# Storing the last two half-groups in parts of 88 and 40 partitions

## The chip, the core and the metric

The kernel runs on one core of a Trainium2 chip. The core has TensorE (PE) for matrix products, VectorE (DVE), ScalarE (ACT) and GpSimd (POOL) for elementwise work, SyncE (SP), which here only issues transfers, and 16 DMA engines that move bytes between the chip's HBM and the on-chip memory SBUF, which has 128 partitions. Every time is device time in microseconds (us), of one whole execution. The kernel before takes 258.17 us, the median of three runs (257.88 to 258.88).

## The reference

Two stages, an attention through 49 agents and a feed-forward layer with a maximum of three products:

```python
def _attn_ref(q, k, v, agents):          # q, k, v: 4 x 12544 x 128, agents: 4 x 49 x 128, float32
    def sm(a, b):                        # softmax of scaled products
        s = scale * (a @ b.transpose(0, 2, 1))
        ...
    agent_v = sm(agents, k) @ v
    return sm(q, agents) @ agent_v

def _moe_ref(x, w1, w2, w3, w_out):      # x: the 50176 rows of the above; w: 128 x 768, w_out: 768 x 128
    h = np.maximum(np.maximum(x @ w1, x @ w2), x @ w3)
    return h @ w_out
```

q, k, v and the output are 25.7 MB each. The output has 50,176 rows of 128 float32.

## The kernel before, in words

Work is cut into tiles of 128 rows: 98 for each of the 4 batches. For each batch, steps of seven tiles of k and v are loaded, cast to bf16 on POOL (for the first batch's v on ACT), turned on PE, and summed into the 49 agents' values. From these the feed-forward layer's products are worked out for each batch once, in the 49 agents rather than in the rows (names nr, pu, pv ... gy).

Then come 49 steps over q, numbered s = 0 to 48. Step s takes a group of eight tiles (the last step, 48, takes the two tiles left over in each batch). A step casts q on POOL (qc), turns it on PE (qt) and copies it out on ACT (qe), multiplies with the agents (sc), exponentiates (ex), sums (su), inverts the sums (re), forms hidden values (u, a, v, x) and the output products (p), and scales these by the inverse sums into an SBUF tile OS: `ov.s.0` writes tiles 0 to 3 of the group, `ov.s.1` tiles 4 to 7. Both run on DVE, but for `ov.47.1`, which runs on ACT as four ACTIVATEs of one tile each (L571), beside DVE's `ov.47.0` (L568).

All large transfers are issued by SyncE on one queue: 40 loads of k and v, 17 of q, 4 of weights and 20 stores, 81 in all, each with all 128 partitions of its tile. The agents alone, 49 partitions, are loaded from ACT's queue (L209). Stores, in `store` (L491 to L498), take three groups at a time (1,536 KB) as long as s is below 45. Steps 45, 46 and 48 are stored alone (512 KB each). Step 47, the last that is worked on, is stored in halves of 256 KB: `st.47.1` after `ov.47.1`, then `st.47.0` after `ov.47.0`. In a half, each partition holds four rows of the output that lie next to each other in HBM, so a partition's part is one run of 4 x 128 x 4 = 2,048 bytes.

The order of all work on all engines is written out by hand in a table of names (`ORDER`), which ends with `st.46 st.47.1 st.47.0`. The names carry the places of their buffers. Eight completion semaphores for transfers (DMAHW0 to DMAHW7) are handed out in turn, so a transfer waits until the one eight issues before it has landed. If too many hidden units stay undecided, another branch (`in_general`) would be taken; it isn't with these inputs. At the end SyncE waits at L754 until each of the eight semaphores shows that its last transfer has landed, and all engines meet in a barrier.

Of the kernel before, what the change touches and what calls it, by code (L numbers as in the profile page):

```python
# [16 lines left out]
P, H, C, A, B, NT, GT, KT, NF = 128, 64, 128, 49, 4, 98, 8, 7, 6  # L17
# [176 lines left out]
class Emit:  # L194
# [296 lines left out]
    def store(self, s, h=None):  # L491
        def fn():
            n = LONG if s < NQ - 1 - TG else GT
            far, near = self.far("out", s, n), self.near(s, self.t[f"os.{s // TG * TG}"], n)
            if h is not None:
                far, near = (x[:, self.tiles(s, h), :] for x in (far, near))
            self.nc.sync.dma_start(far, near)
        return fn  # L498

# [259 lines left out]
```

## Time and profile before

| | |
|---|---|
| median of three runs | 258.17 us |
| the profiled execution | 257.99 us, its span 256.2 us |
| busy share: PE, DVE, ACT, POOL | 76%, 63%, 56%, 57% |
| moved on the large queue q1 | 104.34 MB in 12,432 packets |
| HBM read and written | 78.74 MB, 25.69 MB |
| over the span | 408 GB/s |

The profile is of one execution. Its times count from the span's start. A DMA share of 1.00 means that all 16 DMA engines are moving bytes. A packet is what one DMA engine moves in one go; a transfer's packets are its partitions' runs of bytes, and one mark of 4 bytes on each engine that took part, by which the transfer's semaphore is raised when that engine is done. SPq, ACTq and so on are the instruction streams' own steps (issues and waits), which don't count as an engine's busy time. In a row of a stretch the columns are the stretch, its length, the busy time of PE, PE's weight loads, DVE, ACT and POOL, the clock granted to PE, the DMA share and GB/s.

### The profile page before, as it was taken

What the parts mean: (1) busy time and instruction counts of PE and PEld (TensorE: products, weight loads), DVE (VectorE), ACT (ScalarE), POOL (GpSimd) and SP (SyncE); (2) the same over time, 40 slices, a digit from 0 to 9 for tenths busy, and PEclk for the clock granted to TensorE, in tenths of its full rate; (3) what the DMA queues carried; (4) which work ended last, traced back from release to release, by engine and by line L of the source; (5) the groups of instructions that cost most, each with busy time, mean ns of one, the idle gap of its engine ahead of it and who ended that gap; (6) DMA issues with size and microseconds to landing.
All of it is one profiled execution on the core that took longest, in us unless ns stands there. A gap on an engine that the chain in (4) does not pass through costs nothing.

```text
span 256.2 us, 8245 instructions
## 1 busy us (share of the span) xinstructions
PE 193.7 (76%) x3441; PEld 146.3 (57%) x3441; DVE 160.4 (63%) x332; ACT 144.0 (56%) x240; POOL 144.9 (57%) x164
## 2 busy tenths in 40 slices
PE   0676676889999569997892998559596699999800
PEld 0565555676778348775672586447475376565400
DVE  5353323658788578887647686807448668888820
ACT  2463455654876567573842675237282568888610
POOL 2414533998788498946864496384791663414000
PEclk9995777599999999999995699959899689999965
DMA  6999999999999999999999999999999999999993
GB/s 259 431 417 421 411 432 422 423 420 417 421 418 428 426 423 420 421 425 423 414 429 430 422 421 430 420 424 427 423 430 425 420 422 427 428 425 406 408 387 128
DMA packets 12682, 105.05 MB, mean 410 GB/s; under 512 B 1304, under 2 KB 2524, under 8 KB 4572
## 3 DMA queue, kind: packets, MB, share of 16 engines
q1 hardware_dynamic: 12432, 104.34, 97.3%
q8 instruction: 29, 0.48, 0.7%
q10 hardware_dynamic: 203, 0.10, 0.2%
q14 instruction: 18, 0.14, 0.1%
HBM read 78.74 MB, written 25.69 MB: 408 GB/s over the span
## 4 chain that ended last, share of the span: by engine, by line
DMA 51%; PE 22%; ACT 9%; POOL 7%; issue 4%; DVE 2%; ACTq 0%; DVEq 0%; POOLq 0%
DMA LD<-in_q_dram 32%; PE psum L271 16%; DMA LD<-in_v_dram 13%; PE psum L303 7%; DMA LD<-in_k_dram 6%; ACT QT L514 4%; POOL VB L298 3%; POOL QB L508 2%; DVE OS L568 2%; ACT AS L547 1%; POOL KB L298 1%; ACT VB L296 1%; ACT EQ L527 1%; ACT w_bf L347 1%; ACT EK L318 1%
## 5 line engine op out<-in xcount | busy, mean ns | idle before, releaser
L508 POOL CAST QB<-LD 128x1024 bf16<-128x1024 f32 x49 | 50.0, 1055 | 48.6 <-DMA LD<-in_q_dram 42.6
L298 POOL CAST KB<-LD 128x896 bf16<-128x896 f32 x56 | 51.2, 947 | 27.4 <-DMA LD<-in_k_dram 25.2
L568 DVE TENSOR_TENSOR OS<-psum,RC 128x512 f32<-128x512 f32 x97 | 61.4, 678 | 8.4 <-PE psum L271 5.7
L514 ACT ACTIVATE QT<-psum 128x1024 bf16<-128x1024 bf16 x49 | 50.2, 1024 | 26.2 <-PE psum L303 26.0
L309 DVE COPY KT<-psum 128x896 bf16<-128x896 bf16 x56 | 34.4, 620 | 38.4 <-PE psum L303 37.5
L298 POOL CAST VB<-LD 128x896 bf16<-128x896 f32 x42 | 38.6, 951 | 8.2 <-DMA LD<-in_v_dram 8.2
L303 PE MATMUL psum<-ident,QB 128*128 128x128 bf16 x392 | 34.5, 239 | 11.0 <-POOL QB L508 11.0
L303 PEld LDWEIGHTS <-QB 128*128 128x128 bf16 x392 | 28.9, 108 | 23.0 <-POOL QB L508 12.5
L527 ACT ACTIVATE EQ<-psum 128x512 bf16<-128x512 f32 x49 | 29.3, 598 | 21.3 <-PE psum L271 19.9
L303 PE MATMUL psum<-ident,KB 128*128 128x128 bf16 x392 | 36.4, 246 | 6.3 <-POOL KB L298 5.8
L271 PE MATMUL psum<-QT,agT 128*128 128x512 bf16 (+1 forms) x104 | 32.6, 403 | 8.7 <-ACT QT L514 8.3
L318 ACT ACTIVATE EK<-psum 128x343 bf16<-128x343 f32 x56 | 24.9, 460 | 25.3 <-PE psum L271 19.7
L550 DVE TENSOR_TENSOR R<-psum,AS 128x512 bf16<-128x512 f32 x49 | 32.7, 678 | 7.1 <-ACT AS L547 6.6
L303 PEld LDWEIGHTS <-KB 128*128 128x128 bf16 x392 | 28.2, 111 | 10.8 <-POOL KB L298 8.3
L547 ACT ACTIVATE AS<-psum 128x512 bf16<-128x512 f32 x49 | 28.6, 600 | 9.5 <-PE psum L271 9.3
L271 PE MATMUL psum<-EQ,G 128*128 128x512 bf16 (+1 forms) x104 | 31.9, 379 | 0.0
L271 PEld LDWEIGHTS <-EQ 49*128 49x128 bf16 (+1 forms) x588 | 20.9, 96 | 11.1 <-ACT EQ L527 4.6
L271 PE MATMUL psum<-EK,VB 128*128 128x49 bf16 x392 | 19.7, 187 | 5.6 <-ACT VB L296 3.9
L271 PEld LDWEIGHTS <-ones 128*128 128x128 bf16 x417 | 17.8, 98 | 8.1 <-issue 3.1
L271 PE MATMUL psum<-EK,ones 128*128 128x49 bf16 x392 | 19.6, 187 | 2.2 <-ACT EK L318 2.2
L271 PE MATMUL psum<-G,EQ 49*128 49x128 bf16 x392 | 19.9, 220 | 0.5 <-DVE OS L568 0.5
L271 PE MATMUL psum<-G,R 64*128 64x128 bf16 x392 | 19.3, 217 | 0.5 <-DVE R L550 0.2
(82 smaller groups left out, 186.9 us busy)
## 6 DMA issues: line engine op xcount, KB each, us to landing
LD<-in_q_dram SPq DMA_DIRECT2D x16, 1536.0 KB, 18.8
out_dram<-OS SPq DMA_DIRECT2D x15, 1536.0 KB, 22.4
LD<-in_k_dram SPq DMA_DIRECT2D x16, 1344.0 KB, 16.7
LD<-in_v_dram SPq DMA_DIRECT2D x16, 1344.0 KB, 17.1
LD<-in_k_dram SPq DMA_DIRECT2D x4, 896.0 KB, 18.5
LD<-in_v_dram SPq DMA_DIRECT2D x4, 896.0 KB, 17.6
out_dram<-OS SPq DMA_DIRECT2D x3, 512.0 KB, 10.4
LD<-in_moe_w_dram SPq DMA_DIRECT2D x3, 384.0 KB, 12.9
```

The costliest lines, as they stand in the source:

```text
L271: self.nc.tensor.matmul(out, w, x, start=start, stop=True, skip_group_check=True)
L296: self.nc.scalar.activation(out, src, AF.Copy)
L298: self.nc.gpsimd.tensor_copy(out=out, in_=src)
L303: self.nc.tensor.transpose(t[:, j * P:(j + 1) * P], src[:, j, :], self.ident)
L309: return lambda: self.nc.vector.tensor_copy(out=self.t[f"kT{r}"], in_=self.t[f"kT_ps{r}"].bitcast(BF16)[:, :KT * C])
L318: return lambda: self.nc.scalar.activation(self.t[f"e{r}"], self.t[f"s{r}"][:, :KT * A], AF.Exp, scale=SCALE)
L508: return lambda: self.nc.gpsimd.tensor_copy(out=self.t[f"qb.{s}"], in_=self.half("q", s))
L514: return lambda: self.nc.scalar.activation(self.t[f"qT.{s}"].rearrange("p j c -> p (j c)"), self.t[f"qT_ps.{s}"].bitcast(BF16), AF.Copy)
L527: return lambda: self.nc.scalar.activation(self.t[f"e.{s}"], self.t[f"qs.{s}"], AF.Exp, scale=SCALE)
L547: return lambda: self.nc.scalar.activation(self.t[f"a.{s}"], self.t[f"u.{s}"], AF.Relu)
L550: return lambda: self.nc.vector.tensor_tensor(out=self.t[f"r.{s}"], in0=self.t[f"v.{s}"], in1=self.t[f"a.{s}"], op=ALU.max)
L568: self.nc.vector.tensor_tensor(out=out, in0=src, in1=rc.unsqueeze(2).to_broadcast([P, 4, C]), op=ALU.mult)
```

## The change

The two stores with a half given (`st.47.1` and `st.47.0`) are each issued as two transfers, partitions 0 to 87 and then 88 to 127, with the same bytes in all. `h` is given for these two alone.

```diff
@@ -494,6 +494,9 @@
             far, near = self.far("out", s, n), self.near(s, self.t[f"os.{s // TG * TG}"], n)
             if h is not None:
                 far, near = (x[:, self.tiles(s, h), :] for x in (far, near))
+                for rows in (slice(0, 88), slice(88, P)):
+                    self.nc.sync.dma_start(far[rows], near[rows])
+                return
             self.nc.sync.dma_start(far, near)
         return fn
```

No other engine's order changes; lines behind L496 are numbered three higher. On SyncE, at the end of the branch that runs, OS_115 is the tile of steps 45 to 47, `128x1024` is a group and `128x512` a half; in brackets stands what a transfer waits for. Before:

```order
L497 DMA out_dram<-OS_117 128x4x256 [waits DMAHW2_49,DVE_49]
L497 DMA out_dram<-OS_116 128x3072 [waits DMAHW3_49,DVE_49]
L497 DMA out_dram<-OS_118 128x3072 [waits DMAHW4_49,DVE_49]
L497 DMA out_dram<-OS_114 128x3072 [waits DMAHW5_49,DVE_49]
L497 DMA out_dram<-OS_115 128x1024 [waits DMAHW6_49,DVE_49]
L497 DMA out_dram<-OS_115 128x1024 [waits DMAHW7_49,DVE_49]
L497 DMA out_dram<-OS_115 128x512 [waits DMAHW0_49,Activation_49]
L497 DMA out_dram<-OS_115 128x512 [waits DMAHW1_49,DVE_49]
L258 UNCONDITIONAL_BRANCH
```

With the change:

```order
L500 DMA out_dram<-OS_117 128x4x256 [waits DMAHW2_49,DVE_49]
L500 DMA out_dram<-OS_116 128x3072 [waits DMAHW3_49,DVE_49]
L500 DMA out_dram<-OS_118 128x3072 [waits DMAHW4_49,DVE_49]
L500 DMA out_dram<-OS_114 128x3072 [waits DMAHW5_49,DVE_49]
L500 DMA out_dram<-OS_115 128x1024 [waits DMAHW6_49,DVE_49]
L500 DMA out_dram<-OS_115 128x1024 [waits DMAHW7_49,DVE_49]
L498 DMA out_dram<-OS_115 88x512 [waits DMAHW0_49,Activation_49]
L498 DMA out_dram<-OS_115 40x512 [waits DMAHW1_49]
L498 DMA out_dram<-OS_115 88x512 [waits DMAHW2_49,DVE_49]
L498 DMA out_dram<-OS_115 40x512 [waits DMAHW3_49]
L258 UNCONDITIONAL_BRANCH
```

Each half has become two rows. The second half's first part takes the semaphore DMAHW2 instead of DMAHW1 and so waits for the store of step 48 (`128x4x256`), and the part behind it takes DMAHW3 and waits for the store after that. The second part of a half waits for no engine, since the first part ahead of it has already done so.

## The prediction

> **What bounds the kernel now.** I read the page's overview of 40 slices first, to see which resource is full over the whole span and which at its end.
>
> ```profile
> span 256.2 us, 8245 instructions
> DMA  6999999999999999999999999999999999999993
> GB/s 259 431 417 421 411 432 422 423 420 417 421 418 428 426 423 420 421 425 423 414 429 430 422 421 430 420 424 427 423 430 425 420 422 427 428 425 406 408 387 128
> ```
>
> The DMA engines are at nine tenths in every slice but the first and the last; moving bytes bounds the kernel. The change touches only the last slice, so I went to its end: the timeline of the three engines that still work there (SPq rows are transfers being issued; third column is the duration, rows of several are merged).
>
> ```profile
> 243.30 1.88 DVE L568 TENSOR_TENSOR OS<-psum,RC 128x512 f32<-128x512 f32 x3
> 243.90 1.14 ACT L571 ACTIVATE OS<-psum,RC 128x128 f32<-128x128 f32 x4 [1.25 <-PE psum L271]
> 244.60 0.33 SPq L497 DMA_DIRECT2D out_dram<-OS  x1
> 245.07 1.14 SPq L497 DMA_DIRECT2D out_dram<-OS  x1
> 246.31 0.97 SPq L497 DMA_DIRECT2D out_dram<-OS  x1
> ```
>
> VectorE and ScalarE finish at 245.2 and 245.0. The last two rows are the two half-group stores: issued from 245.07 and 246.31, the second done issuing at 247.28. What happens between there and 256.2 is shown by the DMA issues of the stretch from 246.25 on (KB, then us from issue to landing) and SyncE's waits there.
>
> ```profile
> out_dram<-OS SPq DMA_DIRECT2D x1, 256.0 KB, 8.6
> ...
> SPq L754 <- DMA out_dram<-OS: 7.5, 2, 6.7
> ```
>
> The last store lands 8.6 us after its issue began, at 246.31 + 8.6 = 254.9; SyncE waits 7.5 us for such landings; 1.3 us of closing follow. 256 KB at the pace of the full slices is well under a microsecond, so nearly all of the 8.6 us is queueing behind earlier stores. How the queue drains decides the case. The stretches of the tail (the last two columns are the DMA share and GB/s; nothing else is busy):
>
> ```profile
> 246.00:248.00 2.00, 0.00 (x0) 0.00 (x0) 0.00 (x0) 0.00 (x0) 0.00 (x0) 0.50 0.99 396
> 250.00:252.00 2.00, 0.00 (x0) 0.00 (x0) 0.00 (x0) 0.00 (x0) 0.00 (x0) 0.50 0.68 269
> 252.25:253.00 0.75, 0.00 (x0) 0.00 (x0) 0.00 (x0) 0.00 (x0) 0.00 (x0) 0.50 0.30 117
> 253.00:253.25 0.25, 0.00 (x0) 0.00 (x0) 0.00 (x0) 0.00 (x0) 0.00 (x0) 0.50 0.28 107
> 253.25:253.75 0.50, 0.00 (x0) 0.00 (x0) 0.00 (x0) 0.00 (x0) 0.00 (x0) 0.50 0.19 74
> 253.75:254.25 0.50, 0.00 (x0) 0.00 (x0) 0.00 (x0) 0.00 (x0) 0.00 (x0) 0.50 0.09 37
> 254.25:256.20 1.95, 0.00 (x0) 0.00 (x0) 0.00 (x0) 0.00 (x0) 0.00 (x0) 0.50 0.00 0
> ```
>
> Times 16, the shares count the engines still working: 16 to 248, about 11 from 250 to 252, 5 from 252.25 to 253, 3 around 253.5, one or two up to 254.25, none after. The 16 engines do not finish together; about five end by 250, six around 252.2, five between 253.1 and 254.2. The kernel ends when the last of them does. Bytes per working engine stay the same throughout: 396 / (0.99 x 16) = 25.0 GB/s at the start, 74 / (0.19 x 16) = 24.3 near the end. A lone engine gets no faster, so a row of 2,048 bytes costs its engine 2,048 / 25.0 = 82 to 2,048 / 24.3 = 84 ns, at any time.
>
> **The change part by part.** First, on how many engines a transfer runs. The table of queues:
>
> ```profile
> q1 hardware_dynamic: 12432, 104.34, 97.3%
> q8 instruction: 29, 0.48, 0.7%
> q10 hardware_dynamic: 203, 0.10, 0.2%
> ```
>
> q10 carries one transfer alone, the agents, 49 partitions with 4 rows of 512 bytes each: 196 packets. 203 - 196 = 7 are left, the completion marks, one for each engine that took part. So 49 partitions went over 7 engines. On q1 each of the 81 transfers (61 loads, 20 stores, all of 128 partitions) leaves 16 marks: 81 x 144 packets, and 2 x 384 more for the two transfers with four rows a partition, are 12,432. The pattern that fits both is the largest number up to 16 that divides the partitions. By it 88 partitions go over 11 engines with 8 rows each, 40 over 10 engines with 4 rows each. This is worked out, not shown: neither shape occurs before.
>
> *Rows on an engine.* A half-group store gave each of 16 engines 8 rows. It now gives ten engines 8 + 4 = 12, one engine 8 and five none, if the smaller sets lie within the larger. Two halves: 8 more rows for ten engines, 0 for one, 16 fewer for five. At 83 ns: +0.66 us, 0, and -1.33 us. There are also two more marks on each of ten engines; of 4 bytes each, I cost them at nothing, with 0.02 us as the upper end.
>
> *Which engine is last.* Five engines are within 1.1 us of the end and the very last, on its own, within some 0.4 us. If it is one of the ten, everything behind it moves by +0.66 us. No view names engines; by count that is 10 of 16.
>
> *Two more issues on SyncE.* A usual issue is 0.33 us (244.60 row); the last two took 1.14 and 0.97. Four issues at 1.14 and about 0.1 us between them end at 245.07 + 4 x 1.24 = 250.0. The engine that ends at 254.2 begins the rows of the last two stores 16 x 0.083 = 1.3 us earlier, at 252.9. So 2.9 us of queued work cover the issues on that engine and I cost them at nothing; if that backlog were gone, the cost would be up to 250.0 - 247.28 = 2.7 us. The engines that run dry by 250 may wait for rows, but have four microseconds to spare.
>
> *Waits.* SyncE's order, shown with the change above, has each transfer wait for the one issued eight before it (its DMAHW semaphore). The second half's wait moves from DMAHW1 to DMAHW2 and its second part waits for DMAHW3, which the store five places ahead of the first half signals. That store's issue, and its time to landing:
>
> ```profile
> 226.19 0.34 SPq L497 DMA_DIRECT2D out_dram<-OS  x1
> ...
> out_dram<-OS SPq DMA_DIRECT2D x1, 1536.0 KB, 16.9
> ```
>
> It lands at 226.19 + 16.9 = 243.1, two microseconds before the first half is issued, and DMAHW2 was issued before it. No new stall. No compute engine waits for these stores, and nothing moves on PE, ACT, DVE or POOL.
>
> *Sum.* 0.66 + 0 + 0 + 0 = +0.66 us, bounds -1.3 (all five late engines spared) and +0.68. The profiled execution took 257.99 us around its span of 256.2, 0.18 under the median 258.17; the span would be 256.9, and the median 258.8.
>
> A rule that speaks against this change: the Trainium skill ("DMA: Bandwidth & Descriptors", section Rules for kernel authors) says not to split a transfer over disjoint sets of partitions, since both parts spray across all 16 engines and serialize. The 7 marks of q10 speak against the "all 16" for a part whose partitions 16 does not divide; by the rule as it stands the change would be a mere second issue, with next to no cost.
>
> **The rivals.**
>
> *The last engine is spared.* If it is one of the five left out, it ends at 254.2 - 1.3 = 252.9 and the next ones decide. The rows have about three working engines until 253.75, so some still end around 253.8; with +0.66 they end at 254.4 to 254.5: +0.25 us, 258.4. For it: 5 in 16 by count; against it: two or three of the late ones would have to be spared before it brings more. The Trainium skill (same page, section Latency and other measured facts) says that engines 7 and 15 are usually slower; if the last one here were 15, this rival would be it. No row here can tell, and I leave a fair chance for it.
>
> *All five late engines are spared.* On the other side of zero: they end by 252.9, the six of 252.2 become last at 252.2 + 0.66 = 252.9, and the gain is 254.2 - 252.9 = 1.3 us: 256.9. It decides only where the set of five left out is the set of five late ones. Instruction fetches (q8: 0.7% of 16 engines' 256.2 us, 29 us in all) could make some engines late and not others, but that picks out no such set.
>
> *The parts go over all 16 engines.* 88 rows are at most 6 on an engine, 40 at most 3: 9 rows for 8, +0.17 us in two halves, 258.3. Against it: 203 packets on q10.
>
> *Slower rows or fewer engines.* Ten or eleven engines might read the same part of SBUF against each other, and no row before has such a store. If the 24 rows on an engine took half as long again, that is +1.0 us more: 259.8. If the number of engines has to be a divisor of 16, both parts go over 8, 16 rows for 8: +1.33 us, 259.5. The seven of q10 speak against the second; the first stays open.
>
> **How the numbers follow.** Last engine among the ten: 0.60, its 10 in 16 with a little taken off for the mechanisms that no row shows. Last one spared: 0.20. All 16: 0.05. All five spared: 0.03. Slower rows or fewer engines: 0.12. I predict the likeliest, 258.8. The range 258.2 to 259.5 leaves out the 0.03 below, part of the 0.12 above, and some room for the median, whose runs spread from 257.88 to 258.88. 0.5%, about what a measurement of this kernel can tell from no change, is 1.3 us: below 256.9 lies hardly half of the five-spared case (0.02); above 259.46 lie most of the slower rows and a little of the first case (0.13); the rest, 0.85, is the same.
>
> **What would show it.** On the page of the changed kernel q1 has 12,432 - 32 + 2 x (11 + 10) = 12,442 packets; 12,464 would mean 16 engines each, 12,432 eight. The issues show two of 176 KB and two of 80 KB in place of two of 256. In the tail the shares should fall below 11 engines from 248 on sooner, and the last working stretch should reach 254.9 in place of 254.2, with the closing 1.3 us unchanged. SyncE's last issue should end by 250. The prediction is wrong if an issue of the last four stands in a wait for a landing, if a row of 2,048 bytes costs other than 83 ns on a working engine, or if the late engines turn out to be the spared ones.

## The result and the profile after

The changed kernel takes 258.47 us (median of 20 runs, 258.04 to 259.04), the kernel before 257.92 us (20 runs beside them, 257.48 to 258.88). The ratio is 1.0022, 95% interval 1.0016 to 1.0028: +0.57 us, between 0.41 and 0.72. It is slower, by less than half a percent. The forecast was +0.66 us. The 258.8 us named with it stood on 258.17 for the kernel before, whose median over these 20 runs is 257.92.

The profiled execution has a span of 256.8 us in place of 256.2. The lines on the span, on the two queues that told how many engines take part, and on the four last issues (those without a third number have no time to landing there):

```profile
span 256.8 us, 8209 instructions
...
q1 hardware_dynamic: 12442, 104.34, 97.2%
...
q10 hardware_dynamic: 203, 0.10, 0.1%
...
out_dram<-OS SPq DMA_DIRECT2D x2, 176.0 KB
out_dram<-OS SPq DMA_DIRECT2D x2, 80.0 KB
```

q1 has ten packets more, as worked out beforehand: two transfers fewer with 16 marks, two more with 11 and two with 10. A sum of packets can't tell 11 and 10 from another pair with the same sum, but the landings recorded on the four parts' semaphores can: behind one increment near the issue there are 11, 10, 11 and 10 of them. The issues on SyncE, and the stretches of the tail (last two columns: DMA share and GB/s), in the same cuts as before up to 254.25:

```profile
245.29 0.92 SPq L498 DMA_DIRECT2D out_dram<-OS  x1
246.27 0.94 SPq L498 DMA_DIRECT2D out_dram<-OS  x1
247.30 0.64 SPq L498 DMA_DIRECT2D out_dram<-OS  x1
247.99 1.02 SPq L498 DMA_DIRECT2D out_dram<-OS  x1
```

```profile
246.00:248.00 2.00, 0.00 (x0) 0.00 (x0) 0.00 (x0) 0.00 (x0) 0.00 (x0) 0.50 1.04 411
250.00:252.00 2.00, 0.00 (x0) 0.00 (x0) 0.00 (x0) 0.00 (x0) 0.00 (x0) 0.50 0.68 265
252.25:253.00 0.75, 0.00 (x0) 0.00 (x0) 0.00 (x0) 0.00 (x0) 0.00 (x0) 0.50 0.41 142
253.00:253.25 0.25, 0.00 (x0) 0.00 (x0) 0.00 (x0) 0.00 (x0) 0.00 (x0) 0.50 0.25 74
253.25:253.75 0.50, 0.00 (x0) 0.00 (x0) 0.00 (x0) 0.00 (x0) 0.00 (x0) 0.50 0.19 57
253.75:254.25 0.50, 0.00 (x0) 0.00 (x0) 0.00 (x0) 0.00 (x0) 0.00 (x0) 0.50 0.13 49
254.25:255.00 0.75, 0.00 (x0) 0.00 (x0) 0.00 (x0) 0.00 (x0) 0.00 (x0) 0.50 0.12 46
255.00:255.25 0.25, 0.00 (x0) 0.00 (x0) 0.00 (x0) 0.00 (x0) 0.00 (x0) 0.50 0.16 49
255.25:256.80 1.55, 0.00 (x0) 0.00 (x0) 0.00 (x0) 0.00 (x0) 0.00 (x0) 0.50 0.00 0
```

Two engines (0.12 x 16) now work on past 254.25, one until 254.98 and one until 255.19; before, no data moved after 254.22. No record names an engine, so an engine is followed here by packets of which one starts where another ends. The one that ends last works through the rows of the four parts from 253.24 to 255.19 without a gap, 24 rows in 1.95 us. Before, the last engine's 16 rows took 1.30 us, from 252.92. The difference, 0.65 us, is the eight rows. The other 0.32 us is there before the halves are reached: 0.22 because this execution comes later to its last stores (the first of the last five stores in the kernel before was issued at 240.60, its like here at 240.82). The rest was not traced; just ahead of the halves a row of 4,096 bytes took 0.55 us, where 0.16 is usual, while an instruction packet moved.

So the last packet ends 0.97 us later, but the span grew by 0.58 only. The last landing came 0.44 us behind the last packet (0.71 before), and the end of the span 1.15 us behind the last landing (1.27 before).

Two things differ from the tail before. Between 253.0 and 253.75 a working engine moves 57 / (0.19 x 16) = 19 GB/s, not 24: of the 256 rows of 2,048 bytes, 18 took more than 97 ns, up to 321, where before none of 256 took more than 91. And SyncE's waits behind the issues:

```profile
SPq L757 <- DMA out_dram<-OS: 0.9, 2, 0.5
SPq L757 <- PEq L757: 0.6, 2, 0.5
```

It waited 7.5 us for landings before and waits 0.9 us now. Its first closing step (the first of the waits for the eight semaphores) comes only at 254.62, though its issues ended at 249.0. The experiments below tell what that is.

### The profile page after: what moved, and what is told of

It reads as the page before. It is cut to its first block, busy times and chain, and to the rows that moved or that the text cites. A ratio compares the mean times of both kernels' runs of the same rounds, so it can differ in the third digit from the quotient of the medians.

```text
span 256.8 us, 8209 instructions
## 1 busy us (share of the span) xinstructions
PE 191.1 (74%) x3403; PEld 147.1 (57%) x3441; DVE 160.4 (62%) x332; ACT 144.1 (56%) x240; POOL 144.6 (56%) x164
## 4 chain that ended last, share of the span: by engine, by line
DMA 51%; PE 22%; ACT 9%; POOL 7%; issue 5%; DVE 2%; ACTq 0%; DVEq 0%; POOLq 0%
DMA LD<-in_q_dram 32%; PE psum L271 15%; DMA LD<-in_v_dram 13%; PE psum L303 7%; DMA LD<-in_k_dram 6%; ACT QT L517 4%; POOL VB L298 3%; POOL QB L511 2%; DVE OS L571 1%; ACT AS L550 1%; POOL KB L298 1%; ACT VB L296 1%; ACT EQ L530 1%; ACT w_bf L347 1%; ACT EK L318 1%
## 5 line engine op out<-in xcount | busy, mean ns | idle before, releaser
L271 PE MATMUL psum<-QT,agT 128*128 128x512 bf16 (+1 forms) x82 | 27.3, 401 | 9.5 <-ACT QT L517 8.5
L271 PE MATMUL psum<-EQ,G 128*128 128x512 bf16 (+1 forms) x88 | 27.2, 383 | 0.4
```

Of the source, the lines that this page charges most:

```text
L271: self.nc.tensor.matmul(out, w, x, start=start, stop=True, skip_group_check=True)
```

## The experiments

The theory is that the last DMA engine decides and that it gets four more rows for each half. The rivals are that more transfers cost by themselves, and that the last engine is spared or rows get slower. All kernels compute and store the whole output; only their transfers differ. Each was compared with the kernel before on the same chip; times are ratios of these, and 1 us is 0.39%.

**As many transfers, no row more.** The cut in the change is replaced:

```diff
-                for rows in (slice(0, 88), slice(88, P)):
-                    self.nc.sync.dma_start(far[rows], near[rows])
+                for a, b in ((0, 64), (64, 128)):
+                    self.nc.sync.dma_start(far[a:b], near[a:b])
```

> The two halves go in parts of 64 and 64 partitions. As many extra issues as in the change, but 64 divides by 16, so all 16 engines keep 4 + 4 = 8 rows of a half. Theory 'rows on the last engine': no more rows, two more marks of 4 bytes; +0.0 us against before (at most +0.1), q1 12,432 + 32 = 12,464 packets. Rival 'the extra transfers cost by themselves' (issue, completion): as much as the change, +0.55 us.

Measured: 1.0007 (0.9997 to 1.0016), +0.18 us (-0.08 to +0.41); q1 12,464 packets. The rival's +0.55 lies outside the interval. The row theory stands, with room for a few tenths beside it. In the profiled execution the data ended at 253.96, no later than before (254.22), though 35 of its 256 rows of 2,048 bytes took over 97 ns. SyncE's first closing step came at 254.69, 0.38 us behind the last landing (254.31).

**Half the change.** Only the last store is cut in 88 + 40:

```diff
-                for rows in (slice(0, 88), slice(88, P)):
+                for rows in (slice(0, 88), slice(88, P)) if h == 0 else (slice(0, P),):
```

> Only the last store (the half of tiles 0 to 3) goes in 88 + 40, the half before it whole. Theory 'rows on the last engine': 4 rows of 83 ns more on it, +0.33 us against before, q1 12,437 packets. Rival 'the extra transfers cost by themselves': also about half, +0.28. Rival 'only the first split half delays, by keeping the second one's issue back': 0.

Measured: 1.0010 (1.0001 to 1.0019), +0.26 us (0.03 to 0.49). It fits half of the change, and excludes barely that the second split costs nothing. It does not tell the rows (+0.33) from the extra transfers (+0.28); of these two runs only the one above does.

**Two cuts with half the rows.** In place of 88 and 40 stand 104 and 24, and in another kernel 72 and 56.

```diff
-                for rows in (slice(0, 88), slice(88, P)):
+                for a, b in ((0, 104), (104, 128)):     # the other kernel: ((0, 72), (72, 128))
```

> Both halves in parts of 104 and 24: 13 engines with 8 rows and 12 with 2, so 10 rows for 8 on twelve engines. Theory 'rows on the last engine': 4 more rows in two halves, half of the change, +0.33 us; q1 12,450 packets. Rival 'the extra transfers cost by themselves': as the change, +0.55.

> Both halves in parts of 72 and 56: 6 + 4 rows on twelve engines, 4 on two. As many rows on the last engine as with 104 + 24 (10 for 8), in another cut. Theory 'rows on the last engine' alone: +0.33 us. If 104 + 24's +0.72 us came from its cut (engines that read partitions which other engines read at the same time), another cut may give another time; if it was chance, both lie at +0.33 to +0.5. q1 12,452 packets.

Measured: 104 + 24: 1.0028 (1.0017 to 1.0040), +0.72 us (0.44 to 1.03). 72 + 56: 1.0020 (1.0010 to 1.0030), +0.52 us (0.26 to 0.77). The second holds the +0.33 of the rows; the first does not, and is no smaller than the whole change. q1 has 12,450 and 12,452 packets, as the engine counts (13 and 12, 12 and 14) give. With 104 + 24 something comes on top of the rows.

**Earlier stores too.** The single-group stores of steps 45 and 46 are cut like the halves:

```diff
-            self.nc.sync.dma_start(far, near)
+            for rows in (slice(0, 88), slice(88, P)) if n == GT and s < NQ - 1 else (slice(0, P),):
+                self.nc.sync.dma_start(far[rows], near[rows])
```

> As the change, and the two single-group stores before the halves (steps 45 and 46, 4,096 bytes a partition) also in 88 + 40. Theory 'rows on the last engine', with the last engine's queue never dry after 241 us: 4 more rows of 4,096 bytes (0.16 us each) for each of the two, +1.3 us on top of the change's +0.6, in all +1.9 us; q1 12,452 packets. Rival 'only what is issued last counts': +0.6. Rival 'the extra transfers cost by themselves': twice the change, +1.1.

Measured: 1.0109 (1.0091 to 1.0126), +2.81 us (2.35 to 3.25), with single runs from 259.88 to 262.37. "Only what is issued last counts" is out, since +0.6 is far below: rows given to the last engine anywhere in its queue cost. But +1.9 is too little. In the profiled execution, the slowest of the six (span 260.6), one engine took 1.90, 0.70, 1.07 and 1.37 us, from 248.40 to 253.47, for four rows of 12,288 bytes of a whole store that usually take 0.46 each, while other engines had gone on to the cut stores. That is 3.2 us more; by its times this is the engine that ended last, and it took up the cut stores' rows at 253.50. So slow rows delayed the last engine in this execution; how much they add to the median was not traced.

**The same four stores in even parts.** `slice(0, 64), slice(64, P)` in the kernel above:

> As e4_groups (steps 45 and 46 and the two halves of 47 all in two parts), but 64 + 64: as many transfers, 16 engines in each, no row more on any engine. Theory 'rows on the last engine' alone: +0.0 us, and e4_groups should then have been +1.9. Rival 'extra transfers, or other engines reading the same partitions, cost': of e4_groups' +2.8 us the part over +1.9, some +0.9 us, shows here too. q1 12,432 + 64 = 12,496 packets.

Measured: 1.0035 (1.0023 to 1.0046), +0.90 us (0.59 to 1.19), with no row more on any engine. That seemed to be the missing 0.9 us, and its rows are slow indeed: 92 of 256 rows of 2,048 bytes took over 97 ns. But the stretches of its tail say otherwise:

```profile
252.00:254.00 2.00, 0.00 (x0) 0.00 (x0) 0.00 (x0) 0.00 (x0) 0.00 (x0) 0.50 0.62 198
254.00:255.00 1.00, 0.00 (x0) 0.00 (x0) 0.00 (x0) 0.00 (x0) 0.00 (x0) 0.50 0.00 0
255.00:256.00 1.00, 0.00 (x0) 0.00 (x0) 0.00 (x0) 0.00 (x0) 0.00 (x0) 0.50 0.03 8
```

The data ends at 254.06, earlier than in the kernel before (254.22), and yet the span is 256.7. Its last landing is at 254.54; SyncE's first closing step at 255.34. Its waits after 247 have one row only, and none for a landing:

```profile
SPq L755 <- PEq L755: 0.6, 2, 0.5
```

So the slow rows were not what ended last in this execution. SyncE was late.

**The same four stores cut along the tiles.** Each part has all 128 partitions and half of the tiles:

```diff
-            self.nc.sync.dma_start(far, near)
+            w = far.shape[1] // 2
+            for j in (slice(0, w), slice(w, 2 * w)) if n == GT and s < NQ - 1 else (slice(0, far.shape[1]),):
+                self.nc.sync.dma_start(far[:, j], near[:, j])
```

> As e8_groups_even, as many transfers (steps 45 and 46 and the two halves of 47 all in two parts), but cut along the tiles: each part has all 128 partitions and half the tiles, so rows are half as long and every partition stays with the engine that reads it in a whole store. Rows per engine double in number with the same bytes: some 6 ns more for each of 32 added packets and 4 more marks, +0.2 us. Theory 'other engines reading the same partitions cost': +0.2 us, and no packet far slower than its kind. Rival 'extra transfers cost by their issue and completion': +0.9 us, as 64 + 64 for the same four stores. q1 12,432 + 4 x (128 + 16) = 13,008 packets.

Measured: 1.0021 (1.0012 to 1.0030), +0.54 us (0.31 to 0.77), between the two and holding neither. Slow rows nearly vanish (11 of 512 of 2,048 bytes, where the cut over partitions had 92 of 256), so it is the cut over partitions that makes most of them. SyncE is late here too: the last landing is at 254.59 and its first closing step at 255.23.

**SyncE late, and nothing else.** In the traces where SyncE's closing begins behind the last landing, a packet of 8 KB on the instruction queue q14 (a fetch of code) ends 1.26 to 1.40 us before it. To separate that from rows, the kernel before gets four, or six, loads of one element behind its last store. Each waits for an older transfer, so that SyncE leaves the branch later:

```diff
             self.nc.sync.dma_start(far, near)
+            for i in range(4) if h == 0 else ():          # the other kernel: range(6)
+                self.nc.sync.dma_start(self.ag_st[:1, 0, i:i + 1], self.io["agents"][0, :1, i:i + 1])
```

> The kernel before, with the last two stores whole, and four loads of one element each issued by SyncE behind them, into a corner of the agents' tile that nobody reads any more. The fourth waits for the last store of three groups, which lands at about 250.4, so SyncE leaves the branch at about 250.9, as in e9_groups_tiles (251.0), and not at 247.4. No row more on any engine (one packet of 4 bytes and a mark each, on one engine). In the traces of 64 + 64, 104 + 24, 72 + 56, 64 + 64 for four stores and the cut along the tiles, SyncE's closing begins later than the last landing, some 1.35 us behind an instruction fetch. Theory 'a late SyncE fetches its closing code late': its closing begins at about 255.2 as there, +0.4 us. Rival 'rows and slow reads alone': +0.0, at most +0.1.

> As e10_tiny4 with six loads of one element; the sixth waits for the second group store, which lands at about 253.4, so SyncE leaves the branch at about 253.9. Theory 'a late SyncE fetches its closing code late': the closing begins at 253.9 + 0.3 to 1.5 us until the fetch starts + 0.3 + 1.35, at 255.9 to 257.0, where before it could begin at once with the landing at 254.0: +1.0 to +2.2 us. Rival 'rows and slow reads alone', with the last small load landing some 1.5 us after its issue, at 255.4: +0.5 us at most.

Measured: four: 1.0012 (1.0003 to 1.0021), +0.31 us (0.08 to 0.54), SyncE out of the branch at 250.83, its first closing step at 254.94. Six: 1.0037 (1.0024 to 1.0051), +0.95 us (0.62 to 1.32), out at 253.41, closing from 256.13, though all data and landings were over by 254.3. With six, its last load's issue, the stretches of the tail and the traffic of 254.5 to 255:

```profile
253.09 0.22 SPq L499 DMA_DIRECT2D ag_st<-in_agents_dram  x1
```

```profile
252.00:254.00 2.00, 0.00 (x0) 0.00 (x0) 0.00 (x0) 0.00 (x0) 0.00 (x0) 0.50 0.29 109
254.00:255.00 1.00, 0.00 (x0) 0.00 (x0) 0.00 (x0) 0.00 (x0) 0.00 (x0) 0.50 0.02 8
255.00:256.00 1.00, 0.00 (x0) 0.00 (x0) 0.00 (x0) 0.00 (x0) 0.00 (x0) 0.50 0.00 0
```

```profile
DMA packets 1, 0.01 MB, mean 16 GB/s; under 512 B 0, under 2 KB 0, under 8 KB 0
...
q14 instruction: 1, 0.01, 3.8%
```

The only thing that moves there is an instruction fetch, from 254.57 to 254.87; 1.26 us later SyncE begins its closing. "Rows and slow reads alone" gave at most +0.5 with six, below the interval; with four its +0.1 lies just inside. A SyncE that leaves its branch late ended the kernel late, with every engine idle. Each of these traces has six such packets behind 247: in the kernel before they start at 247.2, 247.4, 250.6, 250.8, 251.8 and 254.2, with six loads at 247.5, 248.1, 250.5, 251.9, 254.6 and 256.7. The one that has moved, from 250.8 to 254.6, is the one ahead of the closing. That it is SyncE's own fetch is the reading that fits its place; no record names its reader. The loads also make SyncE's code longer, and a kernel with as much code and no delay was not run.

**Many more rows.** Two cuts with small engine counts:

```diff
-                for rows in (slice(0, 88), slice(88, P)):
+                for a, b in ((0, 49), (49, 98), (98, 128)):     # the other kernel: ((0, 63), (63, 126), (126, 128))
```

> Both halves in parts of 49, 49 and 30 partitions: by the largest divisor up to 16, 7 + 7 rows on engines 0 to 6, 2 more on 0 to 14: 16 rows on seven engines for 8, 2 on eight. Theory 'rows on the last engine': if the last one is among the seven that every smaller set holds, 16 more rows of 83 ns in two halves, +1.33 us; if it is one of the next three, it ends 1.0 us earlier, and only the others of the seven count: below +1.0 us. Rival 'the extra transfers cost by themselves' (4 more issues): +0.3 to +0.4, from what 64 + 64 with two more showed. q1 12,432 - 32 + 2 x (7 + 7 + 15) = 12,458 packets.

> Both halves in parts of 63, 63 and 2: 7 + 7 rows on nine engines, 1 more on two of them: 14 or 15 rows for 8, none on seven engines. Theory 'rows on the last engine': +12 rows if it is among the nine, +1.0 us (+1.16 if it is one of the first two); if it is the tenth, about +0.6, from the next behind it. q1 12,432 - 32 + 2 x 20 = 12,440 packets. Together with 49 + 49 + 30 this tells whether the last engine is one of the first seven, of the next two, or the tenth.

Measured: 49 + 49 + 30: 1.0067 (1.0050 to 1.0085), +1.73 us (1.29 to 2.19). 63 + 63 + 2: 1.0070 (1.0057 to 1.0083), +1.81 us (1.47 to 2.14). q1 has 12,458 and 12,440 packets, both as worked out. The first holds +1.33 and not the "below +1.0" of a last engine outside the first seven; a second engine that is nearly as late, with a few tenths on top, could still give the lower end. The second is 0.5 to 1.1 us over its +1.0 (0.3 to 1.0 over the +1.16). In its profiled execution the last engine's two rows of 4,096 bytes ahead of the halves took 0.79 and 0.60 us in place of 0.16 each; in the kernel before one such row took 0.40 late in the tail. How much of the excess these rows are was not worked out.

## Why the prediction was right, point by point

*Engine counts.* 11 and 10 hold, and the largest divisor up to 16 gives the packets on q1 to the last one in every cut (13 and 12, 12 and 14, 7 and 15, 9 and 2 engines). The rival that each part goes over all 16 falls for 88 and 40. The Trainium skill ("DMA: Bandwidth & Descriptors", section Rules for kernel authors) advises against splitting a transfer over disjoint partition halves, since both spread over all 16 engines. Halves of 64 do so here, by their 12,464 packets, and cost +0.18 us with zero inside the interval; for 88 and 40 that ground does not hold.

*Rows on an engine, and the last engine among the ten.* +0.66 us was forecast, 0.41 to 0.72 measured, 0.65 in the last engine's own packets. Half the change gave +0.26. The rivals with a spared last engine gave +0.25 or a gain, both outside the interval, and the engine that ended last had 24 rows, so it was one of the ten. What the Trainium skill says of slower engines 7 and 15 ("DMA: Bandwidth & Descriptors", section Latency and other measured facts) supported the rival less than the prediction has it: the page calls it specific to transfers whose descriptors GpSimd's software makes, and these stores are issued by SyncE.

*The sum.* The rows were sized right. That the sum met the median to 0.1 us is partly luck. The closing was taken as unchanged, but the last store's semaphore is now the fourth of the eight that SyncE waits for, not the second, so two steps of 0.06 us fewer follow the last landing, and this saves 0.12. And by their medians, seven of the eight other cuts over partitions cost 0.2 to 0.9 us more than their rows; the sum had no term for that, and the change showed next to none.

*Two more issues at no cost, 2.9 us of cover.* The sum's zero held, but not for the reason given. The cover was worked out up to the last engine's rows at 252.9. What runs out first, as the small loads are read here, is SyncE's own way: it must be out of the branch early enough to have its closing code before the last landing. In the change it was out at 249.10, and its closing began at 254.62, 0.6 us ahead of the third semaphore's last landing (255.22) and 1.0 ahead of the fourth's (255.63), both of which it waited for. With small loads and no rows, leaving at 250.83 cost +0.31 us, and at 253.41 +0.95. The time of leaving does not settle it alone: 72 + 56, out at 250.08, began its closing at 255.91. The bound "up to 2.7 us, if the issues end at 250.0" named the wrong work as cover.

*Waits.* Right: no issue stood in a wait for a landing. The four took 0.64 to 1.02 us each and ended at 249.0, inside the 250 that was given.

*Slower rows.* The rival was given 0.12 and is real, as a side effect. "A row of 2,048 bytes costs other than 83 ns" was named as a sign of being wrong, and it held for 18 of 256 rows. None was among the 24 of the last engine; three (222 to 293 ns) were on the one that ended 0.21 us before it. With four stores in 88 + 40 slow rows delayed the last engine itself, in the execution that was traced.

*What would show it.* The last working stretch reached 255.2, not 254.9, for the 0.3 us by which the last engine came later to the halves. That engines would fall below 11 sooner did not show: the share from 250 to 252 is 0.68 in both. That spared and loaded engines offset each other there would explain it, but was not traced. The issues of 176 and 80 KB are as foretold; the closing was 1.15 us, not 1.3.

Left open is why 104 + 24 cost as much as the change. In its profiled execution the last landing came 0.26 us later than before, and SyncE's closing 0.26 us after that, out of the branch at 250.34. That accounts for that execution, whose time (258.58) is near the median (258.51), but what delays SyncE there was not tested.

## What to carry to other kernels

At an end where the DMA queue is the limit, the time is that of the last DMA engine, so count rows on an engine and not bytes in a transfer: in these cuts a partition count that 16 does not divide went to fewer engines, and the rows that this added on the last engine were paid in full, 80 to 84 ns for each 2,048 bytes. The issuer's last issue has a deadline of its own, which no landing shows: as these traces read, the code that it runs next is still to be fetched. A tail with idle engines, no landing in the waits and a lone instruction packet is the sign of it.

## What the runs showed that was not expected

Cutting a store over partitions slows some rows: none of 256 rows of 2,048 bytes took over 97 ns before, 18 in the change, 92 with four stores in 64 + 64, while a cut along the tiles left 11 of 512. In whole stores a partition's rows seem to stay with one engine, in cut ones with others, so that two engines read the same place at once; that cause is argued from the pattern and is not shown.

Between leaving the branch and the first closing step SyncE took 2.7 us with six loads, when few engines were still busy, and 3.4 to 5.8 us when it left earlier (64 + 64 for four stores 3.4, four loads 4.1, 104 + 24 5.1, the change 5.5, 72 + 56 5.8), and in that time the traces show no wait of SyncE for a landing.
